# A state-space convolution fused with a gated MLP: convolution over two half-sequences with 2048-point spectra, lag tables of 16 powers by 41 offsets, a new static order

## The chip, the cores and the metric

The kernel runs on one core of one Trainium2 chip. The metric is the device time of one execution in microseconds. Each statement about time rests on several executions of both kernels on the same chip. A single core shows no second die to compare with, so a run counts as slow when it is more than 1.5% above the fastest run of the same kernel. Different runs were made on different chips, each beside the kernel before, so compare two runs by their ratios rather than by their times.

Engine names as in the profile: PE is TensorE, the matrix engine (PEld its weight loads), DVE is VectorE, ACT is ScalarE, POOL is GpSimd, SP the engine that issues most of the DMAs. A trailing q (SPq) is an engine's instruction queue.

## The reference, cut to what matters

```python
def reference(u, A, B, C, log_dt, Dskip, w_gate, w_up, w_down):   # cut: complex A, B, C as re and im
    xn = layernorm(u)                                  # 2048 x 512
    dt = exp(log_dt)[:, None]
    P  = exp((dt * A)[:, :, None] * arange(2048))      # 512 channels x 128 modes x 2048 lags
    K  = einsum("dn,dnl,dn->dl", C, P, dt * B).real    # the convolution kernel: 512 x 2048
    y  = irfft(rfft(pad(xn.T)) * rfft(pad(K)))[:, :2048].T + xn * Dskip
    h  = sigmoid(xn @ w_gate) * (xn @ w_up)            # 512 -> 1792
    return u + y + h @ w_down
```

The kernel splits this into three strands that share the engines:

- **Tables.** K is built from powers. A table G (powers times coefficients) and a table H (offsets) are grown by complex multiplications on DVE, in four chunks of 128 channels. PE multiplies G with H to get all lags ("lag products"), and a selection matmul puts them in order.
- **Units.** In 16 units (2 passes over the channels, 8 units each) PE transforms a slice of the input, forms the spectrum of K with matmuls against constant weights E ("spectrum matmuls"), DVE multiplies the two, and PE transforms back ("inverse matmuls"). Slices go through DRAM between the steps (z before, v after).
- **The gated MLP.** PE does gate, up and down matmuls. DVE multiplies gate and up ("gated products").

## The kernel before: the parts that the argument touches

Every engine is given its instructions in a fixed order. A list `ORDER` of about 900 operation numbers, written in the file, says in which order all operations are issued. It was found by a search before the kernel was written down; no scheduler runs on the chip.

```python
NGE = 32            # powers in G
NH = 21             # offsets in H
ORDER = [ ... ]     # the static order of all operations (cut)

def cmul(lo, outp, n, m, conj, ...):       # n table elements at a time, on DVE
    V.tensor_tensor(out=outp, in0=lo, in1=mre, op=ALU.mult)      # L660
    V.tensor_tensor(out=tmp,  in0=lo, in1=mim, op=ALU.mult)      # L661
    V.tensor_tensor(out=outp[re], ...)                           # L665
    V.tensor_tensor(out=outp[im], ...)                           # L666

def f_k(...):                              # lag products: 64-column tiles, 42 moving columns
    for comp in range(2):
        for t in range(2):
            T.matmul(pk[64*t:64*t+64, y % 8, :], G[:, r, :, comp, h], H[:, r, :, comp, h],
                     start=(comp == 0), stop=(comp == 1), tile_position=(0, 64*t))    # L724
...
for p in range(2):
    for u in range(8):                     # one unit
        lx = dma("SP", zx, z_v[...], acq=[xsl, zsl], ...)        # load of z, 256 KB
        mm = pl.add("PE", ..., fm, [lx, l_m2], ...)              # input transform
        le = dma("SP", es, cten["E"].ap()[:, gs, :, :], ...)(640 * KB)
        def fk(...):                       # 4 groups x 5 = 20 spectrum matmuls    # L810
            for r in range(GB):
                for kt in range(NKT):
                    T.matmul(two(sk)[:, DW*r:DW*r+DW], es()[:, r, kt, :], kT[p][:, kt, :],
                             start=kt == 0, stop=kt == NKT - 1)
        def fp(...):                       # the one product of the unit, 128x2048    # L817
            V.tensor_tensor(out=pp(), in0=xx(), in1=kb(), op=ALU.mult)
        ...                                # 16 inverse matmuls                    # L827
```

Of the kernel before, what the change touches and what calls it, by code (L numbers as in the profile page):

```python
# [31 lines left out]
NGE = 32  # L32
NH = 21
# [3 lines left out]
QUAD = ((0, 0), (2, 64), (1, 0), (3, 64))  # L37
# [16 lines left out]
LAG0 = [0, 1, 2, 3, 4, 5, 6, 7, 258, 260, 262, 516, 772, 256, 512, 768, 1024, 1280, 1536, 1792, 2048]  # L54
# [5 lines left out]
def _th(s, b, k2):  # L60
    return 2 * np.pi * (s * b / 4096.0 + k2 * b / 32.0)

def _build_S1():
    S1 = np.zeros((NA, 128))
    a = np.arange(NA)
    S1[:, 0] = 1.0
    S1[:, 1] = (-1.0) ** a
    for s in range(1, 64):
        S1[:, 2 * s] = np.cos(2 * np.pi * s * a / 128)
        S1[:, 2 * s + 1] = -np.sin(2 * np.pi * s * a / 128)  # L70
    return S1

def _build_S2():
    S2 = np.zeros((128, NA))
    a = np.arange(NA)
    S2[0, :] = 1.0 / 4096
    S2[1, :] = (-1.0) ** a / 4096
    for s in range(1, 64):
        S2[2 * s, :] = 2.0 / 4096 * np.cos(2 * np.pi * s * a / 128)
        S2[2 * s + 1, :] = -2.0 / 4096 * np.sin(2 * np.pi * s * a / 128)  # L80
    return S2

def _build_M2():
    M2 = np.zeros((NG, 128, 128))
    b = np.arange(32)[:, None]
    k2 = np.arange(32)[None, :]
    for g in range(NG):
        for par in range(2):
# [3 lines left out]
            if s >= 1:  # L92
                t = _th(s, b, k2)
                M[0:32, 0:32] = np.cos(t)
                M[32:64, 0:32] = np.sin(t)
                M[0:32, 32:64] = -np.sin(t)
                M[32:64, 32:64] = np.cos(t)
            else:
                t0 = 2 * np.pi * k2 * b / 32.0
                M[0:32, 0:16] = np.cos(t0)[:, 0:16]  # L100
                M[0:32, 32 + 1:32 + 16] = -np.sin(t0)[:, 1:16]
                M[0:32, 32 + 0] = (-1.0) ** b[:, 0]
                t64 = 2 * np.pi * (64 + 128 * (k2 - 16)) * b / 4096.0
                M[32:64, 16:32] = np.cos(t64)[:, 16:32]
                M[32:64, 32 + 16:32 + 32] = -np.sin(t64)[:, 16:32]
# [3 lines left out]
def _build_MAB():  # L109
    MA = np.zeros((NG, 128, 128))  # L110
    MB = np.zeros((NG, 128, 128))
    k2 = np.arange(32)[:, None]
    b = np.arange(32)[None, :]
    for g in range(NG):
        for par in range(2):
# [14 lines left out]
            else:  # L130
# [7 lines left out]
                t64 = 2 * np.pi * (64 + 128 * (k2 - 16)) * b / 4096.0  # L138
# [8 lines left out]
def _row(l):  # L147

    v = int(np.float32(ml_dtypes.bfloat16(l)))
    seg = range(0, 8) if v < 256 else (8, 9, 10, 13) if v < 512 else (11, 12, 14, 15) if v < 1024 else \  # L150
        (16, 17, 18, 19) if v < 2048 else (20,)
    for h in seg:
        if v >= LAG0[h] and (v - LAG0[h]) % 8 == 0 and (v - LAG0[h]) // 8 < NGE:
            return h, (v - LAG0[h]) // 8
    raise ValueError(l)

def _build_E(S1, M2):

    E = np.zeros((NKT, 4, NGE, NG, 128))
    z = M2.reshape(NG, 2, 2, 32, 128)  # L160
    s1 = S1.reshape(NA, NG, 2, 2)
    for l in range(L):
        h, i = _row(l)
        if h < 20:
            E[h // 4, h % 4, i] += np.einsum("gpc,gpcf->gf", s1[l // 32], z[:, :, :, l % 32, :])
    E = E.reshape(NKT, 128, NG, 128).transpose(1, 2, 0, 3)
    for g in range(NG):
        if g % GB >= GB // 2:
            E[:, g] = np.roll(E[:, g], 64, axis=-1)
    return E  # L170

def _consts():
# [4 lines left out]
    def quads(m, cross=False):  # L177
        m = m.transpose(1, 0, 2)
        lo, hi = m[0:64, :, 0:64].copy(), m[64:128, :, 64:128].copy()
        for g in range(NG):  # L180
            if cross and g % GB >= GB // 2:
                lo[:, g], hi[:, g] = m[64:128, g, 64:128], m[0:64, g, 0:64]
# [3 lines left out]
    return dict(ident=f(np.eye(128)), S1=f(np.concatenate([S1, S1], axis=0)), S2=f(_build_S2()), M2=f(quads(M2)),  # L186
# [3 lines left out]
    35, 3, 2, 22, 1, 33, 0, 12, 7, 36, 5, 34, 6, 47, 4, 29, 46, 38, 48, 49, 8, 32, 37, 50, 30, 39, 40, 11, 52, 51, 53, 41, 43,  # L190
    55, 16, 42, 31, 9, 54, 44, 56, 28, 57, 45, 10, 58, 59, 13, 186, 60, 18, 23, 602, 24, 607, 62, 603, 17, 608, 26, 612, 604,
    61, 14, 613, 19, 15, 614, 63, 21, 609, 629, 66, 25, 625, 27, 64, 630, 20, 621, 65, 617, 622, 67, 187, 633, 626, 618, 127,
    637, 68, 126, 645, 634, 128, 638, 641, 125, 646, 70, 69, 138, 130, 141, 653, 642, 99, 71, 657, 100, 654, 102, 635, 72, 73,
    647, 658, 636, 659, 139, 648, 639, 129, 140, 74, 101, 605, 660, 104, 103, 75, 640, 627, 606, 142, 623, 105, 188, 107, 628,
    143, 631, 624, 108, 610, 189, 106, 632, 156, 109, 131, 76, 150, 655, 133, 110, 132, 611, 643, 115, 77, 651, 656, 78, 644,
    649, 79, 151, 615, 650, 190, 152, 159, 80, 619, 652, 111, 616, 160, 191, 177, 135, 620, 161, 82, 134, 661, 81, 136, 112,
    178, 113, 192, 83, 179, 183, 662, 85, 663, 84, 193, 87, 114, 86, 194, 117, 116, 697, 157, 699, 664, 158, 88, 698, 665, 671,
    137, 195, 89, 90, 91, 184, 153, 196, 705, 672, 185, 666, 92, 673, 93, 94, 154, 197, 95, 155, 174, 707, 700, 674, 97, 706,
    675, 683, 96, 708, 681, 200, 203, 243, 198, 206, 689, 202, 682, 205, 691, 204, 690, 180, 216, 201, 729, 98, 676, 692, 199,
    731, 244, 359, 730, 709, 249, 684, 181, 732, 711, 207, 217, 182, 710, 208, 713, 118, 175, 209, 214, 717, 121, 712, 176, 215,  # L200
    719, 714, 210, 119, 693, 718, 211, 120, 701, 220, 122, 165, 720, 162, 702, 123, 221, 703, 694, 212, 163, 715, 704, 246, 164,
    733, 247, 213, 250, 248, 259, 721, 166, 716, 260, 725, 734, 167, 218, 722, 219, 695, 245, 251, 124, 726, 252, 222, 257, 696,
    258, 253, 224, 223, 254, 263, 264, 685, 255, 230, 286, 225, 687, 231, 287, 686, 256, 723, 289, 232, 288, 688, 293, 727, 290,
    233, 291, 292, 735, 261, 234, 168, 728, 171, 235, 757, 169, 172, 226, 170, 736, 765, 236, 758, 173, 227, 724, 767, 228, 237,
    737, 229, 238, 759, 262, 738, 239, 147, 144, 739, 148, 145, 149, 760, 240, 146, 302, 807, 241, 740, 747, 741, 303, 242, 374,
    458, 300, 265, 381, 748, 301, 294, 465, 742, 295, 306, 267, 266, 307, 296, 297, 375, 268, 329, 298, 749, 444, 273, 376, 299,
    274, 333, 304, 378, 334, 275, 330, 377, 305, 332, 337, 335, 380, 459, 336, 276, 269, 766, 379, 338, 460, 775, 768, 270, 345,
    464, 773, 277, 331, 463, 271, 346, 750, 445, 272, 461, 278, 466, 774, 751, 462, 446, 339, 449, 279, 450, 382, 467, 451, 776,
    447, 280, 448, 752, 789, 437, 791, 468, 790, 805, 281, 383, 430, 469, 806, 452, 384, 470, 282, 416, 471, 385, 423, 453, 809,
    808, 386, 431, 454, 761, 810, 387, 432, 283, 388, 455, 762, 434, 417, 763, 792, 433, 418, 284, 436, 781, 456, 421, 438, 419,  # L210
    782, 457, 764, 420, 285, 435, 424, 439, 367, 340, 422, 343, 344, 341, 389, 409, 799, 390, 342, 349, 797, 393, 440, 308, 394,
    798, 391, 800, 425, 360, 350, 392, 441, 426, 309, 801, 442, 347, 402, 427, 348, 802, 443, 310, 428, 429, 361, 316, 783, 311,
    317, 318, 362, 787, 319, 784, 366, 368, 363, 320, 321, 365, 364, 793, 322, 395, 369, 323, 795, 794, 803, 403, 312, 804, 404,
    324, 785, 313, 408, 410, 314, 796, 406, 786, 370, 407, 405, 788, 486, 865, 315, 411, 493, 325, 371, 866, 396, 372, 412, 373,
    326, 570, 811, 397, 577, 413, 812, 487, 398, 833, 414, 488, 777, 415, 327, 556, 399, 778, 489, 779, 492, 400, 328, 490, 769,
    401, 571, 780, 491, 770, 351, 572, 576, 353, 574, 352, 573, 575, 557, 354, 771, 594, 558, 596, 355, 600, 772, 841, 559, 356,
    562, 357, 837, 358, 561, 584, 586, 578, 585, 590, 598, 592, 494, 560, 579, 563, 580, 588, 813, 479, 495, 472, 496, 514, 581,
    814, 497, 582, 815, 498, 583, 499, 564, 816, 817, 473, 521, 565, 823, 474, 566, 475, 500, 477, 515, 818, 824, 480, 476, 516,
    478, 519, 518, 522, 481, 520, 517, 535, 482, 501, 507, 825, 502, 528, 523, 505, 503, 504, 506, 483, 834, 567, 826, 524, 838,
    849, 827, 842, 542, 484, 867, 850, 508, 485, 868, 568, 569, 529, 828, 549, 509, 875, 530, 510, 857, 533, 543, 858, 511, 534,  # L220
    544, 873, 532, 512, 531, 536, 548, 874, 513, 876, 545, 547, 550, 537, 546, 538, 845, 551, 539, 846, 525, 552, 540, 881, 526,
    541, 553, 882, 847, 527, 869, 848, 885, 870, 835, 886, 554, 859, 836, 839, 555, 860, 890, 843, 840, 889, 883, 844, 851, 884,
# [57 lines left out]
def _d1(n):  # L280
    return 0.09 + n * 0.00117
# [737 lines left out]
```

## Time and profile before

The kernel before took 265.56 us (three runs, 264.41 to 265.71); the profiled span is 262.9 us.

| what | before |
|---|---|
| time (median of 3) | 265.56 us |
| span of the profiled run | 262.9 us |
| granted PE clock, mean | 0.993 |
| DMA | 49.34 MB |

The first part of its page gives busy time of each engine, share of the span, and instructions:

```profile
PE 243.0 (92%) x2254; PEld 131.4 (50%) x2254; DVE 192.9 (73%) x389; ACT 157.9 (60%) x247; POOL 21.7 (8%) x41
```

PE is the busiest, but the average hides two stages. The windows view of the kernel before splits the span at the last table instruction. Columns: window, its length, busy time (and instruction count) of each engine, granted PE clock, DMA share, GB/s:

```profile
4.10:171.20 167.10, 155.80 (x1434) 82.05 (x1432) 160.95 (x347) 122.87 (x203) 17.63 (x31) 1.00 0.70 190
171.20:262.90 91.70, 84.50 (x816) 48.36 (x814) 31.94 (x43) 33.87 (x45) 3.27 (x4) 0.98 0.65 186
```

Until the last table is done, DVE is busy 160.95 of 167.10 us. It leaves 6.2 us idle. After it, PE is busy 84.50 of 91.70 us, with 7.2 us idle, 6.3 of them after its last matmul. So this identity holds by construction:

span = 4.1 + (DVE work before the last table + DVE gaps) + (PE work after it + PE gaps)

The waits view of PE in that second stage shows how full it is. Columns: who waited for whom, total us, times, longest:

```profile
PE pair_64 L810 <- DMA big<-c_E: 0.3, 1, 0.3
PE pair_63 L794 <- DMA big<-z_scr: 0.3, 1, 0.3
PE pair_63 L724 <- DVE big L666: 0.3, 1, 0.3
```

PE waits less than one microsecond in all for anything. The same view for DVE in the first stage (the longest wait of its first line, 4.2 us, ends at the stage's start and is no part of the 6.2 us):

```profile
DVE stats L482 <- DMA big<-in_A_u_dram: 4.4, 2, 4.2
DVE big L660 <- ACT big L682: 2.6, 1, 2.6
DVE big L570 <- ACT big L563: 0.7, 1, 0.7
```

The timeline of PE shows what the pieces cost (start, us, engine, line, operation, count):

```profile
135.68 2.35 PE L810 MATMUL pair_64<-big 128*128 128x256 bf16 x20
...
142.31 2.13 PE L724 MATMUL pair_64<-big 128*64 128x42 bf16 x64
...
146.68 0.63 PE L827 MATMUL pair_64<-big 64*64 64x256 bf16 x16
```

### The profile page before, as it was taken

Reading aid. Unit: us, or ns where it says so; the run is one execution under the profiler, and the core shown is the slowest. Engines: PE = TensorE matmul, PEld = TensorE weight load, DVE = VectorE, ACT = ScalarE, POOL = GpSimd, SP = SyncE. Lnnn points to the kernel's source line nnn. Section 1 sums busy time; section 2 is a strip of 40 time slices with the busy share of each in tenths; the row PEclk is TensorE's granted clock in tenths of the full one; section 3 lists DMA queues with packets and bytes.
Section 4 is the critical chain, followed back from the end, with each engine's and each line's share of the span. In section 5 each row is a group of like instructions: output and inputs, shape, how many; then the busy total and the mean of one; then the engine's idle time right before and its main releaser. Section 6 shows DMA issues by size and latency. Waiting matters only on the chain.

```text
span 262.9 us, 5705 instructions
## 1 busy us (share of the span) xinstructions
PE 243.0 (92%) x2254; PEld 131.4 (50%) x2254; DVE 192.9 (73%) x389; ACT 157.9 (60%) x247; POOL 21.7 (8%) x41
## 2 busy tenths in 40 slices
PE   7689998899999989989999999999999999999990
PEld 2353333334336444747567557477457656444440
DVE  3889999999999999999999599924111223566323
ACT  2699999999996544294674845752536776310000
POOL 1300220072000000102000000000020200000000
PEclk9999999999999999999999999999999999999997
DMA  7999975664559022857978846947997983496123
GB/s 163 161 295 323 339 220 145 190 139 107 145 202 157 15 80 80 228 178 143 306 216 253 228 118 193 271 124 235 302 306 175 308 261 96 131 264 201 44 67 100
DMA packets 50924, 49.34 MB, mean 188 GB/s; under 512 B 13137, under 2 KB 44114, under 8 KB 50770
## 3 DMA queue, kind: packets, MB, share of 16 engines
q1 hardware_dynamic: 47362, 44.66, 60.0%
q0 software_dynamic: 960, 1.57, 3.7%
q10 hardware_dynamic: 2576, 2.75, 3.6%
q8 instruction: 17, 0.28, 0.4%
q14 instruction: 9, 0.07, 0.1%
HBM read 30.36 MB, written 12.06 MB: 161 GB/s over the span
## 4 chain that ended last, share of the span: by engine, by line
DVE 47%; PE 28%; DMA 11%; SPq 4%; issue 3%; ACT 3%; DVEq 1%; POOL 1%; ACTq 0%
DVE big L661 8%; DVE big L660 8%; DVE hT_sb L928 8%; DVE big L665 5%; DVE big L666 5%; PE bank_68 L946 5%; SPq L382 4%; PE pair_64 L810 3%; DVE stats L482 3%; DMA big<-z_scr 3%; DMA big<-c_E 2%; DVE big L611 2%; PE bank_67 L921 2%; DMA big<-v_scr_94 2%; DVE big L609 2%
## 5 line engine op out<-in xcount | busy, mean ns | idle before, releaser
L946 PE MATMUL bank_68<-wd_sb,hT_sb 128*128 128x512 bf16 x196 | 44.7, 379 | 1.3 <-ACT glu_sb L976 1.1
L817 DVE TENSOR_TENSOR big<-big 128x2048 bf16<-128x2048 bf16 x16 | 19.5, 1220 | 26.7 <-ACT big L813 15.6
L906 PEld LDWEIGHTS <-wg_sb 128*128 128x128 bf16 x236 | 21.9, 97 | 29.1 <-issue 8.7
L921 PEld LDWEIGHTS <-wu_sb 128*128 128x128 bf16 x224 | 21.0, 97 | 28.8 <-issue 6.5
L946 PEld LDWEIGHTS <-hT_sb 128*128 128x128 bf16 x224 | 21.1, 98 | 27.6 <-issue 3.9
L810 PEld LDWEIGHTS <-big 128*128 128x128 bf16 x320 | 30.8, 98 | 6.7 <-DMA big<-c_E 1.4
L660 DVE TENSOR_TENSOR big<-big 128x256 bf16<-128x256 bf16 (+4 forms) x52 | 31.2, 600 | 2.8 <-ACT big L682 2.6
L661 DVE TENSOR_TENSOR big<-big 128x256 bf16<-128x256 bf16 (+4 forms) x52 | 31.3, 601 | 0.0
L921 PE MATMUL bank_67<-xnT,wu_sb 128*128 128x512 bf16 x88 | 22.6, 379 | 0.3 <-DVE hT_sb L928 0.2
L665 DVE TENSOR_TENSOR big<-big 128x128 bf16<-128x128 bf16 (+4 forms) x52 | 21.4, 412 | 0.6
L810 PE MATMUL pair_64<-big 128*128 128x256 bf16 x180 | 21.2, 273 | 0.6 <-DMA big<-c_E 0.6
L666 DVE TENSOR_TENSOR big<-big 128x128 bf16<-128x128 bf16 (+4 forms) x52 | 21.2, 407 | 0.0
L906 PE MATMUL bank_65<-xnT,wg_sb 128*128 128x512 bf16 (+1 forms) x80 | 19.7, 368 | 1.3 <-ACT hT_sb L915 0.9
L906 PE MATMUL bank_67<-xnT,wg_sb 128*128 128x512 bf16 (+1 forms) x76 | 18.5, 368 | 2.2 <-DVE hT_sb L928 2.2
L928 DVE TENSOR_TENSOR hT_sb<-hT_sb,bank_67 128x512 bf16<-128x512 bf16 x22 | 15.0, 682 | 7.4 <-PE bank_67 L921 7.3
L906 PE MATMUL bank_66<-xnT,wg_sb 128*128 128x512 bf16 (+1 forms) x80 | 19.7, 369 | 0.7 <-DVE hT_sb L928 0.4
L921 PE MATMUL bank_66<-xnT,wu_sb 128*128 128x512 bf16 x72 | 18.5, 380 | 0.2 <-ACT hT_sb L915 0.2
L921 PE MATMUL bank_65<-xnT,wu_sb 128*128 128x512 bf16 x64 | 16.4, 379 | 1.1 <-ACT hT_sb L915 0.5
L928 DVE TENSOR_TENSOR hT_sb<-hT_sb,bank_66 128x512 bf16<-128x512 bf16 x18 | 12.3, 681 | 6.7 <-PE bank_66 L921 3.8
L724 PEld LDWEIGHTS <-big 128*64 128x64 bf16 x512 | 16.1, 157 | 2.2 <-DVE big L666 1.0
L813 ACT ACTIVATE big<-pair_64 128x1024 bf16<-128x1024 f32 x9 | 9.2, 1023 | 13.3 <-PE pair_64 L810 11.1
L915 ACT ACTIVATE hT_sb<-bank_66 128x512 bf16<-128x512 f32 x19 | 11.7, 615 | 8.0 <-PE bank_66 L906 8.0
(117 smaller groups left out, 356.2 us busy)
## 6 DMA issues: line engine op xcount, KB each, us to landing
big<-c_E SPq DMA_DIRECT2D x16, 640.0 KB, 5.7
z_scr<-big SPq DMA_DIRECT2D x16, 256.0 KB, 2.8
big<-z_scr SPq DMA_DIRECT2D x16, 256.0 KB, 5.2
big<-big SPq DMA_DIRECT2D x64, 64.0 KB, 3.3
big<-in_A_u_dram SPq DMA_DIRECT2D x8, 256.0 KB, 7.5
v_scr_94<-big SPq DMA_DIRECT2D x8, 256.0 KB, 3.3
big<-v_scr_94 SPq DMA_DIRECT2D x8, 256.0 KB, 4.6
v_scr_95<-big SPq DMA_DIRECT2D x8, 256.0 KB, 4.0
```

The source lines that it names most:

```text
L660: V.tensor_tensor(out=wide(outp), in0=lov, in1=mre, op=ALU.mult)
L661: V.tensor_tensor(out=wide(tb()), in0=lov, in1=mim, op=ALU.mult)
L665: V.tensor_tensor(out=outp[:, :, :, 0, :], in0=outp[:, :, :, 0, :], in1=tb()[:, :, :, 1, :], op=opr)
L666: V.tensor_tensor(out=outp[:, :, :, 1, :], in0=outp[:, :, :, 1, :], in1=tb()[:, :, :, 0, :], op=opi)
L724: T.matmul(pk[64 * t:64 * t + 64, y % 8, :], G[:, r, :, comp, h], H[:, r, :, comp, h], start=(comp == 0), stop=(comp == 1), tile_position= ...
L810: T.matmul(two(sk)[:, DW * r:DW * r + DW], es()[:, r, kt, :], kT[p][:, kt, :], start=kt == 0, stop=kt == NKT - 1)
L817: V.tensor_tensor(out=pp().rearrange("p c g d -> p c (g d)"), in0=xx().rearrange("p c g d -> p c (g d)"), in1=kb().unsqueeze(1).to_broadca ...
L906: T.matmul(bank(sl)[:, c0:c1], w[:, kt, k * 128:(k + 1) * 128], xnT[:, grp, kt, c0:c1], start=(kt == 0), stop=(kt == KT - 1))
L915: S.activation(out=hT_sb[:, hs.idx, k % 2, :], in_=bank(sl), func=ACT.Sigmoid)
L921: T.matmul(bank(sl), wu_sb[:, kt, k * 128:(k + 1) * 128], xnT[:, grp, kt, :], start=(kt == 0), stop=(kt == KT - 1))
L928: V.tensor_tensor(out=h(), in0=h(), in1=bank(sl), op=ALU.mult)
L946: T.matmul(bank(po), hT_sb[:, hts[k // 2].idx, k % 2, jj * 128:(jj + 1) * 128], wd_sb[:, k, :], start=(k == 0), stop=k == FT - 1, **kw)
```

## The change

The intent: two half-sequences make each spectrum 2048 points instead of 4096, so the spectrum matmuls and their constant weights halve (PE and DMA are relieved). For that, each unit needs one more product on DVE and more inverse matmuls. The lag tables become 16 powers by 41 offsets, so the lag products sit on 32-column tiles with 82 moving columns. The order of all operations was searched anew.

```diff
-NGE = 32
-NH = 21
+NGE = 16
+NH = 41
+NU = 16
 ... (constants of the transforms for 2048 points cut)
-ORDER = [ ... ]
+ORDER = [ ... another list, for the new set of 930 operations ... ]
 def f_k(...):
-    for t in range(2):
-        T.matmul(pk[64*t:64*t+64, y % 8, :], G[:, r, :, comp, h], H[:, r, :, comp, h], ...,
-                 tile_position=(0, 64*t))
+    for t in range(4):
+        T.matmul(pk[32*t:32*t+32, y % 4, :], G[:, r, :, comp, h], H[:, r, :, comp, h], ...,
+                 tile_position=(0, 32*t))
 ...
-le = dma("SP", es, cten["E"].ap()[:, gs, :, :], ...)(640 * KB)
+le = dma("SP", es, cten["E"].ap()[:, gs, :, :], ...)(320 * KB)
 def fk(...):
-    for r in range(GB):                 # 4 groups
+    for g in range(2):                  # 2 groups
         for kt in range(NKT): T.matmul(...)
 ...
+def fpb(...):                            # second product of the unit, 128x1024
+    V.tensor_tensor(out=pq(), in0=xx()[:, :, 0, :], in1=kb()[:, 2*DW:4*DW]..., op=ALU.mult)
+pb_ = pl.add("DVE", 0.62, fpb, [pa_], ...)
 ...                                      # inverse matmuls: 16 -> 24 per unit
```

Not shown: the selection was rewritten for the new tables, and some buffers were added (spectrum weights 2 to 3, the evicted spectrum of K 1 to 2).

## The prediction

> What bounds it now. The windows view gives two stages. From 4.1 to 171.5 us VectorE (DVE) is busy 161.3 of 167.4 us, TensorE (PE) 155.8. It ends with the last DVE table instruction, after which PE starts the last lag-table product. From 171.5 to 262.9 us DVE is busy 31.6 of 91.4 us, PE 84.5: PE-bound, with 6 us of finals and stores at the end. So the span is (DVE work before the last table) + (PE work after it) + gaps. PE's clock row is full; the clock plays no part.
>
> What changes, with pitches from the timeline:
> - Kernel-spectrum matmuls halve, 320 to 160; twenty take 2.18 us, so PE drops 34.9 to 17.5 us. Their DMA (16 x 640 KB) halves.
> - Lag-table matmuls stay 512, on 32-column tiles instead of 64, with 82 moving columns instead of 42. Today 64 take 2.08 to 2.3 us (33 ns each), more than streaming needs[...]. The selection matmuls, with 32-column weights, take 13.5 ns. The Trainium skill, "TensorE: Matmul & The Clock Gate" (LDWEIGHTS), says load time follows the weight's columns; the trace agrees in direction. Estimate 0.9 to 1.0 us per 64: 17.5 to 7.5 us over eight.
> - Inverse matmuls grow 256 to 384: 16 take 0.57 us, 24 about 0.85; +4.5 us. Selection +1 us.
> - PE pitches sum to 230 us before, about 209 after (-21).
> - DVE: table steps are 47 instead of 44 elements per chunk (+4 us); each unit gets a second product, 128x1024, about 0.6 us, x16 = +10 us. Sum 191 to 206 us.
> - ScalarE hardly changes.
>
> Critical path. I placed both static instruction orders against these pitches. Before: 161 us of DVE work up to the last table instruction (ended at 172: 10 us of gaps), then 81 us of PE work, 4 of gaps, 6 of tail: 262.9. After: 172 us of DVE work up to the last table instruction (table elements, eight second products, three more gated products), then 65 us of PE work. The second stage gains 16 us, the first loses 11: only 5 of 21 us survive at equal gaps. PE gets some 30 us of slack in the first stage, which gains nothing. I expect 2 to 4 us less DVE stall early (layer-norm statistics come first in its queue), a tail 1 us shorter, and 2 to 5 us more PE wait behind the last inverse matmul, where 8 us of other PE work covers the store and reload of the result (3 to 4 and 4.6 to 6.5 us to landing today).
> Lower bound: 4 + 172 + 65 + 5 = 246 us of span; the stated time is about 2.7 us above the span today.
>
> Predicted: 256.0 us, range 248.0 to 264.0. Faster by over 2%: 0.74; within 2%: 0.22; slower: 0.04.
>
> What the profile would show. Last table instruction at 178 to 184 us, DVE 95% busy before it, PE clearly under its present 93% there; DVE busy 203 to 210 us in all, PE near 222; 64 lag matmuls in 0.85 to 1.1 us; 10 spectrum matmuls in 1.1; 24 inverse ones near 0.85; first final matmul 48 to 58 us after the last table; DMA near 43 MB.
>
> What would make it wrong. If the last table comes well before 178 us, or less PE work follows it, time falls to 248 or below. If 32-column tiles do not beat 33 ns, 2 us are lost behind the tables and the rest is hidden. If DVE waits for swapped copies or ScalarE (three 0.9 us evictions per unit), or the reload stalls PE by 8 us, it ends near 264.

## The result, and the profile after

The changed kernel took 278.98 us (four runs, 276.59 to 280.86), the kernel before in the same rounds 265.63 us (four runs, 264.41 to 267.98). The ratio is 1.045, with a 95% interval of 1.036 to 1.054: slower by 4.5%. A ratio here is always the mean time of one kernel's fast runs over that of the other's fast runs of the same rounds, so it is not quite the ratio of the medians that I quote.

The page of the changed kernel, engine totals:

```profile
PE 229.2 (83%) x2290; PEld 117.6 (43%) x2290; DVE 208.6 (76%) x407; ACT 162.7 (59%) x249; POOL 20.8 (8%) x43
```

PE lost 14 us of busy time and DVE gained 16. DMA went from 49.34 to 43.42 MB. The windows view of the changed kernel, split again at its last table instruction:

```profile
4.10:193.00 188.90, 156.97 (x1511) 77.77 (x1508) 174.07 (x354) 129.61 (x209) 15.75 (x31) 0.96 0.57 153
193.00:276.00 83.00, 69.50 (x778) 38.80 (x774) 34.51 (x54) 31.89 (x40) 3.27 (x4) 0.97 0.62 169
```

| | before | changed | difference |
|---|---|---|---|
| DVE work up to the last table | 160.95 | 174.07 | +13.1 |
| DVE gaps there | 6.2 | 14.8 | +8.6 |
| PE work after it | 84.5 | 69.5 | -15.0 |
| PE gaps there | 7.2 | 13.5 | +6.3 |
| span, with 4.1 us at the start | 262.9 | 276.0 | +13.1 |

The work terms alone would have given 1.9 us. The gaps cost 14.9 us. That is the result in one line. One caution: each column is one execution, and the one of the kernel before is a quick one (its 35 executions beside the experiments have spans of 262.8 to 267.4 us, half of them 264.6 or less). So some 2 us of the 14.9 may be the draw, and a difference of 2 or 3 us in one gap should not be read.

The waits of DVE in the first stage, changed kernel (4.1 us of its first line end at the stage's start again):

```profile
DVE stats L499 <- DMA big<-in_A_u_dram: 5.4, 3, 4.1
DVE hT_sb L964 <- PE bank L957: 2.8, 4, 1.6
DVE ln_nb_f L472 <- ACT ln_m_f L467: 2.7, 2, 1.4
DVE big L841 <- DMA big<-big: 1.8, 1, 1.8
DVE big L680 <- ACT big L721: 1.4, 2, 1.1
```

Two of them lie in the first 20 us (the input and the layer-norm means). From 20 us on DVE waits 7.2 us instead of 2.6: for the matmuls of the gated products, for the swapped copies of the transformed input, for ScalarE.

The pieces on PE's timeline in the changed kernel (two lines whose bracket names the wait before them):

```profile
140.31 1.25 PE L835 MATMUL pair<-big 128*128 128x256 bf16 x10 [0.35 <-ACT big L837]
141.50 0.85 PE L858 MATMUL pair<-big 64*64 64x256 bf16 x24
...
192.78 2.88 PE L744 MATMUL pair<-big 128*32 128x82 bf16 x128 [2.59 <-DVE big L685]
```

Ten spectrum matmuls and 24 inverse matmuls take what was predicted (the listed lengths overlap a little; the next piece starts 0.1 to 0.2 us before they end). The lag products do not: 128 take 2.7 to 2.9 us, 21 to 23 ns each, where 15 had been assumed.

The waits of PE around and after the last table, in the changed kernel:

```profile
PE pair L817 <- DMA big<-z_scr: 4.3, 2, 3.6
PE pair L744 <- DVE big L685: 2.6, 1, 2.6
PE bank L908 <- DMA big<-v_scr: 1.7, 1, 1.7
PE pair L858 <- DVE big L841: 1.5, 1, 1.5
PE bank L957 <- DVE hT_sb L964: 0.7, 2, 0.5
```

The wait of 2.6 us for the table ends at 192.78 us and so lies before the split at 193.0. The others, 8.2 us against 0.9 before, lie in the second stage: for z loads, for the reload of v in the tail, and for DVE. The idle time at the very end is 1 us shorter than before (5.3 us), as predicted.

One more thing is new. The clock row of the page before is full until the last slice. In the changed kernel PE falls to about half its clock several times. One of these places, in the timeline of PE, with the wait for a z load in the bracket:

```profile
178.33 0.64 PE L817 MATMUL pair<-big,m 64*64 64x256 bf16 x8 [2.82 <-DMA big<-z_scr]
178.90 1.89 PE L942 MATMUL bank<-xnT,wg_sb 128*128 128x512 bf16 x4
180.72 1.27 PE L766 MATMUL pair<-big,sw 128*32 128x96 bf16 x64
181.93 1.04 PE L957 MATMUL bank<-xnT,wu_sb 128*128 128x512 bf16 x4
```

After 2.82 us of idle time four matmuls of 512 columns take 1.89 us, and a little later four take 1.04 us. The windows view (same columns as above) confirms the clock there, at 0.53 to 0.55 in three such stretches:

```profile
62.00:65.60 3.60, 2.83 (x7) 0.99 (x7) 3.57 (x7) 3.57 (x6) 0.00 (x0) 0.53 0.41 143
178.20:181.80 3.60, 3.47 (x76) 1.70 (x76) 3.13 (x7) 1.02 (x1) 0.00 (x0) 0.53 0.08 18
222.70:226.40 3.70, 3.70 (x16) 1.92 (x15) 1.27 (x2) 1.91 (x3) 0.00 (x0) 0.55 0.64 168
```

The Trainium skill, "TensorE: Matmul & The Clock Gate" (Why this matters for your kernels), warns of PE-idle gaps above about 3 us between bursts of matmuls, because an idle window takes the array back to half its clock. This trace agrees in kind, but the length of the gap alone does not decide it. Gaps of 2.7 and 2.8 us were enough here (before 62.8 and 178.3 us), while one of 2.8 us before 135.6 us and one of 2.6 us before 192.8 us left the clock at 1.00. No run here shows what else decides.

### The profile page after: what moved, and what is told of

Read it like the earlier page. It is cut to its first block, busy times and chain, and to the rows that moved or that the text cites. A ratio compares the mean times of both kernels' runs of the same rounds, so it can differ in the third digit from the quotient of the medians.

```text
span 276.0 us, 5805 instructions
## 1 busy us (share of the span) xinstructions
PE 229.2 (83%) x2290; PEld 117.6 (43%) x2290; DVE 208.6 (76%) x407; ACT 162.7 (59%) x249; POOL 20.8 (8%) x43
## 2 busy tenths in 40 slices
DMA packets 51069, 43.42 MB, mean 157 GB/s; under 512 B 13153, under 2 KB 44258, under 8 KB 51042
## 4 chain that ended last, share of the span: by engine, by line
PE 40%; DVE 29%; DMA 16%; ACT 6%; issue 4%; SPq 2%; DVEq 0%; ACTq 0%
PE bank L942 11%; PE bank L957 9%; DMA big<-z_scr 8%; PE bank L982 6%; DVE big L681 5%; DVE big L680 5%; PE pair L744 4%; DVE hT_sb L964 4%; PE pair L835 4%; DVE big L685 4%; DVE big L686 3%; DMA ident<-c_ident 3%; DMA big<-big 2%; DMA big<-v_scr 2%; SPq L397 2%
## 5 line engine op out<-in xcount | busy, mean ns | idle before, releaser
L942 PE MATMUL bank<-xnT,wg_sb 128*128 128x512 bf16 (+1 forms) x236 | 57.4, 382 | 1.4 <-ACT hT_sb L951 1.4
L957 PE MATMUL bank<-xnT,wu_sb 128*128 128x512 bf16 x224 | 55.9, 384 | 2.9 <-ACT hT_sb L951 1.5
L982 PE MATMUL bank<-wd_sb,hT_sb 128*128 128x512 bf16 x224 | 52.2, 387 | 3.3 <-ACT glu_sb L1012 3.3
L964 DVE TENSOR_TENSOR hT_sb<-hT_sb,bank 128x512 bf16<-128x512 bf16 x56 | 37.0, 682 | 10.7 <-PE bank L957 6.0
L951 ACT ACTIVATE hT_sb<-bank 128x512 bf16<-128x512 f32 x56 | 32.3, 599 | 15.1 <-PE bank L942 15.0
L680 DVE TENSOR_TENSOR big<-big 128x256 bf16<-128x256 bf16 (+5 forms) x52 | 33.1, 636 | 2.5 <-ACT big L721 1.4
L681 DVE TENSOR_TENSOR big<-big 128x256 bf16<-128x256 bf16 (+5 forms) x52 | 32.9, 633 | 0.0
L822 ACT ACTIVATE big<-pair 128x1024 bf16<-128x1024 f32 x16 | 16.3, 1026 | 11.4 <-PE pair L817 7.3
L685 DVE TENSOR_TENSOR big<-big 128x128 bf16<-128x128 bf16 (+5 forms) x52 | 21.9, 420 | 0.8
L835 PE MATMUL pair<-big 128*128 128x256 bf16 x160 | 20.4, 278 | 2.2 <-ACT big L837 0.7
L862 ACT ACTIVATE big<-pair 128x1024 bf16<-128x1024 f32 x16 | 16.4, 1026 | 9.0 <-PE pair L858 5.2
L686 DVE TENSOR_TENSOR big<-big 128x128 bf16<-128x128 bf16 (+5 forms) x52 | 21.6, 416 | 0.0
L837 ACT ACTIVATE big<-pair 128x1024 bf16<-128x1024 f32 x16 | 16.4, 1027 | 7.8 <-PE pair L835 3.4
L835 PEld LDWEIGHTS <-big 128*128 128x128 bf16 x160 | 15.9, 100 | 8.2 <-issue 3.0
L645 ACT ACTIVATE big<-pair 128x1024 bf16<-128x1024 f32 x16 | 16.3, 1019 | 1.7 <-DMA z_scr<-big 1.0
L858 PE MATMUL pair<-big 64*64 64x256 bf16 x384 | 13.7, 272 | 3.1 <-ACT big L822 1.6
## 6 DMA issues: line engine op xcount, KB each, us to landing
z_scr<-big SPq DMA_DIRECT2D x16, 256.0 KB, 2.6
big<-z_scr SPq DMA_DIRECT2D x16, 256.0 KB, 4.6
v_scr<-big SPq DMA_DIRECT2D x16, 256.0 KB, 2.6
big<-v_scr SPq DMA_DIRECT2D x12, 256.0 KB, 4.6
big<-in_A_u_dram SPq DMA_DIRECT2D x8, 256.0 KB, 7.2
```

Of the source, the lines that this page charges most:

```text
L680: V.tensor_tensor(out=wide(outp), in0=lov, in1=mre, op=ALU.mult)
L681: V.tensor_tensor(out=wide(tb()), in0=lov, in1=mim, op=ALU.mult)
L685: V.tensor_tensor(out=outp[:, :, :, 0, :], in0=outp[:, :, :, 0, :], in1=tb()[:, :, :, 1, :], op=opr)
L686: V.tensor_tensor(out=outp[:, :, :, 1, :], in0=outp[:, :, :, 1, :], in1=tb()[:, :, :, 0, :], op=opi)
L835: T.matmul(two(sk)[:, o:o + DW], es()[:, g, kt, :], kT[p][:, kt, :], start=kt in (0, NKT - 1), stop=kt >= NKT - 2)
L942: T.matmul(bank(sl)[:, c0:c1], w[:, kt, k * 128:(k + 1) * 128], xnT[:, grp, kt, c0:c1], start=(kt == 0), stop=(kt == KT - 1))
```

## The experiments

Two theories at the start. **Order:** the new operations are worth about what was predicted, but the list in which they stand wastes it in waits, and another list of the same operations is fast. **Work:** the new set of operations is itself no better, because PE's saved work lies where it does not count and DVE's added work where it does. A third question is whether the lost **clock** is a cause or a shadow of the waits.

All times are medians of four runs, slow ones included; beside each stands the ratio to the kernel before of the same rounds, with its 95% interval.

| run | us | ratio | 95% interval |
|---|---|---|---|
| changed kernel | 278.98 | 1.045 | 1.036 to 1.054 |
| e1_start | 278.58 | 1.044 | 1.036 to 1.052 |
| e2_tail | 274.80 | 1.028 | 1.021 to 1.035 |
| e3_zload | 273.98 | 1.029 | 1.022 to 1.036 |
| e4_all | 276.89 | 1.040 | 1.032 to 1.049 |
| e5_after_reordered | 265.84 | 1.003 | 0.996 to 1.011 |
| e6_before_reordered | 270.16 | 1.011 | 1.004 to 1.019 |
| e7_spectra_doubled | 278.30 | 1.046 | 1.041 to 1.051 |
| e8_before_half_spectra | 268.54 | 1.009 | 1.004 to 1.014 |
| e9_before_extra_dve | 274.29 | 1.026 | 1.018 to 1.034 |
| e10_before_half_spectra_half_load | 261.40 | 0.978 | 0.971 to 0.986 |
| e11_reordered_start_a | 271.74 | 1.015 | 1.007 to 1.024 |
| e12_reordered_start_b | 274.73 | 1.026 | 1.018 to 1.034 |
| e13_kept_clock | 277.23 | 1.033 | 1.025 to 1.042 |
| e14_second_product_gpsimd | 286.39 | 1.078 | 1.072 to 1.084 |
| e15_reordered_gpsimd | 278.79 | 1.044 | 1.033 to 1.055 |
| e16_reordered_other_seed | 269.41 | 1.013 | 1.005 to 1.020 |
| e17_zload_and_tail | 276.25 | 1.037 | 1.030 to 1.043 |
| e18_reordered_one_move | 266.31 | 1.000 | 0.995 to 1.005 |

And the two-stage sum, worked out from the windows view of the profiled run of each, split at that run's last table instruction:

| run | last table at | DVE work + gaps before it | PE work + gaps after it | span | mean clock |
|---|---|---|---|---|---|
| before | 171.2 | 161.0 + 6.2 | 84.5 + 7.2 | 262.9 | 0.993 |
| changed kernel | 193.0 | 174.1 + 14.8 | 69.5 + 13.5 | 276.0 | 0.965 |
| e5_after_reordered | 188.2 | 172.2 + 11.9 | 72.3 + 6.9 | 267.4 | 0.984 |
| e7_spectra_doubled | 191.4 | 174.1 + 13.2 | 75.2 + 9.3 | 275.9 | 0.987 |
| e8_before_half_spectra | 174.6 | 161.0 + 9.5 | 78.9 + 13.7 | 267.2 | 0.958 |
| e9_before_extra_dve | 178.3 | 166.5 + 7.7 | 84.9 + 8.8 | 272.0 | 0.986 |
| e10_before_half_spectra_half_load | 173.6 | 161.0 + 8.6 | 76.4 + 8.9 | 258.9 | 0.971 |
| e18_reordered_one_move | 185.5 | 172.2 + 9.2 | 72.9 + 6.3 | 264.7 | 0.991 |

(The profiled run of e5 was its slowest, 269.45 us; its other three lie at 265.7 to 265.9. So its gaps are on the high side, as those of the kernel before are on the low side.)

### e1_start, e2_tail, e3_zload, e4_all: repairing single waits of the changed kernel

```diff
 # e1: loads of the identity and log_dt earlier, the warm-up matmuls all at the start
+_mv([7, 6], 2); _mv([30, 31, 32, 33, 34, 35, 36, 37], 29)     # move operations in ORDER behind another
 # e2: in the tail, reloads of v stand ahead of the output stores in the queues
+_mv([604, 616, 612, 605], 608); _mv([610, 606], 618)
 # e3: a z load needs only its own buffer, and five of them are issued earlier
-lx = dma("SP", zx, ..., acq=[xsl, zsl]);  ex = pl.add("ACT", 0.91, fe, [mm])
+lx = dma("SP", zx, ..., acq=[zsl]);       ex = pl.add("ACT", 0.91, fe, [mm], acq=[xsl])
+_mv([571], 497); _mv([541], 482); _mv([556], 572); _mv([586], 542); _mv([526], 557)
 # e4: all three
```

> Only the issue order of the start changes: the identity and log_dt loads go right behind the first four input loads, and all 30 warm-up matmuls run first. Order theory (the new order, not the new work, costs the time): transposes start near 10.5 us instead of 12.7, TensorE is at full clock when the first gate matmuls start, the first lag-table product starts 3 to 5 us earlier than 90.8, total 3 to 5 us less than the changed kernel (about 274 to 276 us). Work theory (the extra VectorE work and the longer chain per unit cost it): a gain at the start is eaten by VectorE later, total within 1 us of the changed kernel.

> Only the issue order of the end changes: the six reloads of the inverse result that stand behind output stores in the DMA queues are issued before the first output store. Order theory: the wait of 1.7 us before the first late final matmul and the 5 us reload in the chain that ended last go, total 2 to 3 us less than the changed kernel. Work theory: less than 1 us.

> The spectrum loads (z) of the last five units no longer wait for a free buffer of the forward result (that buffer is taken at the eviction instead) and are issued right behind the matmul that frees their own buffer. Order theory: after the last lag-table product the products of those five units come less than 5 us apart instead of 6.6, TensorE waits for z fall from 4.3 to under 1 us in that stage, total 4 to 8 us less. Rival: the chain of eviction, swapped copies and product sets that pace, not the load; then the waits move to the swapped copies and the total changes by under 2 us.

> The three order edits together. Order theory: gains add, 9 to 16 us, 262 to 269 us, near the kernel before. Work theory: at most 3 us, 275 us or more.

The repaired start gained nothing: 278.6 us, although the last table came 2.8 us earlier in its profiled run (190.2 us); PE's gaps behind it grew from 13.5 to 16.0 us. The tail and the z loads each gained 1.6 to 1.7%, some 4 to 5 us. All three together gained less than either of these alone, with intervals that overlap. A single wait taken away is real, but what it sets free runs into the next one. The traces show it: in e3 PE's waits for z after the last table go from 4.3 us to none, and its waits for the DVE product before the inverse matmuls from 1.5 to 4.1 us.

### e17_zload_and_tail: only the two repairs that worked

```diff
+ the edits of e2 and of e3 together, not that of e1
```

> The changed kernel with the two repairs that each gave 4 to 5 us (earlier z loads; reloads ahead of the stores in the tail), without the third, the early start, which alone gave nothing. If they lie on separate stretches of the path and the start was what spoilt the run with all three (276.9 us): 269 to 271 us. If any shift of the order upsets the rest: 273 to 278 us.

276.25 us. The two do not add either. Their ratios alone were 1.028 and 1.029, together 1.037. The intervals overlap, so I do not say that the pair is worse than one of them; I say that a second 4 us did not appear. In its trace the waits for z are down to 0.5 us and those for the DVE product up to 3.8 us. The losses of this order are not separate waits that can be struck off one by one.

### e5_after_reordered and e6_before_reordered: the same operations in another list

```diff
-ORDER = [ ... ]     # the list of the kernel
+ORDER = [ ... ]     # the same numbers in another sequence, from a local search over a rough model
```

The search moves one to four operations at a time and keeps what shortens a model made of measured durations, dependences, buffers and waits for DMA. It was run in the same way on both kernels, started from the kernel's own list or from an earlier result of the search.

> The changed kernel with every operation kept and only the list of the static order replaced by one found by a local search over the two pieces of the work (durations from the traces, eight DMA lanes, waits). Theory A (the new list, not the new work, makes the kernel slow): 258 to 266 us, at or below the kernel before, granted clock above 0.98, last table instruction by 186 us. Theory B (the new work itself is slower: 13 us more VectorE work in stage one and small pieces that nothing can cover): it stays above 272 us whatever the order.

> The kernel before, operations kept, its order replaced by one from the same search. It is the fair partner of the reordered changed kernel. If the order of the kernel before was already good: 262 to 268 us, the same as the kernel before. If the search finds something general that the hand-in order lacks: 255 to 260 us. If the search only fits its own rough durations: above 270 us.

The changed kernel in its new list took 265.84 us, 13 us less than in its own (11 us by the ratios, 1.003 against 1.045), and the same as the kernel before. The kernel before in a searched list took 270.16 us: its own list was no worse than what the search found. (Only one searched list was run for it, against four for the changed kernel.) So the search is no magic, and the list that came with the change was a bad one for these operations. The windows view of e5, split at its last table:

```profile
4.10:188.20 184.10, 150.01 (x1469) 74.97 (x1493) 172.17 (x349) 127.29 (x206) 13.10 (x28) 0.98 0.55 153
188.20:267.40 79.20, 72.27 (x797) 40.98 (x804) 37.19 (x58) 31.14 (x41) 5.75 (x7) 0.99 0.68 187
```

PE's gaps after the last table went from 13.5 to 6.9 us; there is 2.8 us more PE work there and it costs nothing extra. One wait is left in that stage:

```profile
PE pair L746 <- DVE big L687: 0.3, 1, 0.3
```

Theory Order holds for 11 to 13 us. It does not hold for the rest: the new operations in the best list tried are not faster than the old ones in theirs.

### e7_spectra_doubled: the saved PE work put back

```diff
-                for g in range(2):
+                for g in (0, 1, 0, 1):          # every spectrum matmul twice, same result
```

> The changed kernel with its spectrum matmuls run twice into the same bank (same result): 17 us of TensorE work put back, 8.7 of it in pass one (before the last table) and 8.7 in pass two. If the saved TensorE work is worth its full length everywhere: +17 us (296). If it is worth something only after the last table, as the prediction holds: +8 to +9 us (287), last table unmoved within 2 us. If stage two too is bound by waits and not by work: +0 to +5 us (279 to 284).

278.30 us: the 17 us of PE work came back for nothing. The windows view of e7:

```profile
4.10:191.40 187.30, 162.16 (x1565) 83.71 (x1584) 174.12 (x354) 129.62 (x208) 15.75 (x31) 0.98 0.58 155
191.40:275.90 84.50, 75.20 (x847) 46.31 (x858) 34.67 (x55) 31.51 (x40) 3.27 (x4) 1.00 0.60 166
```

In the second stage busy time rose by 5.7 us, less than the 8.7 us of matmuls added, in part because the clock there is 1.00 instead of 0.97; and the gaps fell by 4.2 us. The clock rose from 0.965 to 0.987. DVE's gaps before the last table hardly moved, 13.2 against 14.8 us. In the changed kernel's own order the halved spectra, its main gain, are worth nothing, in the first stage as predicted and in the second stage against the prediction.

### e8 and e10: the gain of the change alone, in the kernel before

```diff
 # e8: 10 of 20 spectrum matmuls (wrong on purpose)
-                    for kt in range(NKT):
+                    for kt in ((0, 1, NKT - 1) if r % 2 else (0, NKT - 1)):
 # e10: 10 matmuls, and only half of the weights loaded
-le = dma("SP", es, cten["E"].ap()[:, gs, :, :], ...)
+le = dma("SP", lambda: es()[:, 0:2], cten["E"].ap()[:, GB*u:GB*u+2, :, :], ...)
-                for r in range(GB): for kt in range(NKT): T.matmul(..., es()[:, r, kt, :], ...)
+                for r in range(GB): for kt in ((0, 1, 2) if r % 2 == 0 else (3, 4)): T.matmul(..., es()[:, r // 2, kt, :], ...)
```

> The kernel before with only 10 of the 20 spectrum matmuls of each unit (wrong result on purpose; loads, order, everything else as before): the gain of the change alone, without its costs. The prediction's sum says 17 us less TensorE work, of which 8.7 lie after the last table: 257 to 258 us. If waits take the place of the work: 261 to 265 us.

> The kernel before with 10 of 20 spectrum matmuls and also only half of the spectrum weights loaded, 16 x 320 KB instead of 16 x 640 KB (wrong result on purpose). The run with half of the matmuls alone took 268.5 us, with waits for these loads among the stage-two waits. If the loads held it: 258 to 262 us, granted clock back above 0.98. If the waits only move to the z loads and to the VectorE and ScalarE hand-overs, and TensorE goes on losing its clock in them: 264 to 269 us.

Both compute a wrong spectrum. The comparison with the reference happened to let e8 pass (the convolution is a small part of the output) and refused e10 with an error of 0.024; neither is a kernel to use.

With half of the spectrum matmuls alone, the kernel before became 0.9% slower. Windows of e8 and, after them, its waits of PE in the second stage:

```profile
4.10:174.60 170.50, 149.92 (x1337) 76.27 (x1352) 160.99 (x347) 122.70 (x202) 17.62 (x31) 0.96 0.67 187
174.60:267.20 92.60, 78.93 (x726) 41.35 (x736) 32.00 (x43) 33.92 (x45) 3.27 (x4) 0.95 0.63 183
```

```profile
PE pair L810 <- DMA big<-c_E: 3.2, 3, 2.1
PE pair L794 <- DMA big<-z_scr: 1.9, 1, 1.9
```

PE's busy time in the second stage fell by 5.6 us only, in part because matmuls after the waits ran at half the clock (14 down matmuls took 4.9 us after the z wait, 3.2 us before it), and the gaps rose by 6.5. The loads now set the pace that PE had set. With the loads halved too, e10 took 261.4 us, 2.2% less than before:

```profile
...
173.60:258.90 85.30, 76.36 (x736) 40.79 (x734) 31.98 (x43) 34.08 (x45) 3.27 (x4) 0.99 0.62 175
```

The wait for the weights is gone from its list; PE gaps are 8.9 us. (The expectation of a clock above 0.98 failed: it is 0.971, with 0.99 in the second stage.) So the change's gain exists and is worth about 6 us in the old order, not the 8.7 us of its matmuls after the last table, and only if the loads shrink with it.

### e9_before_extra_dve: the main cost of the change alone, in the kernel before

```diff
                 V.tensor_tensor(out=pp(), in0=xx(), in1=kb(), op=ALU.mult)
+                V.tensor_tensor(out=pp()[:, 0], in0=xx()[:, 0], in1=kb(), op=ALU.mult)   # same values again
```

> The kernel before, with one more 128x1024 VectorE product after each of its 16 products (it rewrites the first half of the result with the same values): the cost of the change's second product alone, 16 x 0.6 us. If VectorE before the last table is the bound of stage one, as the prediction says, those that stand before it (5 to 8) move the last table and the end by 3 to 5 us: 269 to 271 us. If VectorE has slack even there: 266 to 267 us. If each product also lengthens the path of its unit in stage two: 273 us or more.

274.29 us, +2.6%: nearly 7 us for 16 products that take 0.6 us each (9.6 us of DVE). The windows view of e9 shows the first stage:

```profile
4.10:178.30 174.20, 156.87 (x1435) 82.81 (x1432) 166.47 (x355) 122.91 (x203) 17.65 (x31) 0.99 0.66 184
178.30:272.00 93.70, 84.89 (x816) 48.49 (x814) 37.53 (x51) 33.86 (x44) 3.27 (x4) 0.98 0.63 180
```

Eight of them stand before the last table (355 instructions instead of 347), add 5.5 us of work there and move it by 7.1 us. DVE work before the last table costs its full length. Most of the other 1.6 us is no effect of the edit: DVE's wait for the input at the start is 5.6 us in this execution and 4.4 us in that of the kernel before.

Put together: in the kernel before, the gain alone (e10) is worth 6 us and this cost alone (e9) takes 7. The table elements, 4.4 us more in the changed kernel's groups of table instructions, come on top. That fits Theory Work: the best list tried for the new operations only equals the old kernel. It is not a proof. The added inverse matmuls were not run alone, the three terms sum to about 5 us of loss that e5 does not show, and a better list may exist.

### e13_kept_clock: dummy matmuls in the waits

```diff
 def fm(...):                                     # input transform of a unit
+    for _ in range(10 if (p, u) in ((0, 3), (1, 1), (1, 5)) else 0):
+        T.matmul(two(sl)[:, 0:512], xnT[:, 0, 0, 0:128], xnT[:, 0, 0, 0:512], start=True, stop=True)
 def f_k(...):                                    # lag products
+    for _ in range(6 if half_ == 0 else 0): T.matmul(...the same...)
```

> The changed kernel in its own order with dummy matmuls that keep TensorE busy where the trace shows it idle for 2.1 to 3.6 us: 10 ahead of three of the unit transforms that wait for their z load, 6 ahead of each chunk's first lag product (about 0.2 us each, into the bank that the operation holds already; same result). They stand in waits, so they cost nothing where the wait is still there. If the clock that TensorE loses after such gaps matters: granted clock 0.98 or more and 3 to 5 us less, 274 to 276 us. If the waits are the matter and the clock only their shadow: clock up, time 277 to 280 us.

The profiled run's clock rose from 0.965 to 0.986. The times were 275.95 and 273.81 us in the two fast runs and 278.52 and 278.67 in two that count as slow, with clocks of 0.986, 0.992, 0.973 and 0.971. Fast runs against fast runs the ratio fell from 1.045 to 1.033, about 3 us, but the two intervals overlap, and with all four runs of each kernel the means lie only some 2 us apart. So the lost clock may be worth some 2 to 3 us of the 23 us by which the prediction missed. It is not settled, and it is not the main cause. A searched list (e16, below) ran at clocks of 0.949 to 0.963, no higher than the changed kernel's, and took 269.4 us. And with the clock kept, the profiled run still has 9.6 us of PE gaps after the last table, dummy matmuls not counted as gaps.

### e14 and e15: the second product on GpSimd

```diff
-                V.tensor_tensor(out=pq(), in0=xx()[:, :, 0, :], ...)
+                P.tensor_tensor(out=pq(), in0=xx()[:, :, 0, :], ...)
-            pb_ = pl.add("DVE", 0.62, fpb, ...)
+            pb_ = pl.add("POOL", 0.62, fpb, ...)
```

> The changed kernel, own order, with the second product on GpSimd instead of VectorE: takes some 10 us off VectorE, 5 of them before the last table. If VectorE's added work is what the change pays with (the same addition cost the kernel before 7 us): 272 to 275 us, last table 4 to 5 us earlier. If GpSimd is slow at it (over 2 us each) and in the way of its own queue: the units' chain grows and it ends at 280 us or later.

> The searched order (265.8 us) with the second product on GpSimd. If VectorE bounds stage one and GpSimd needs under 2 us: 260 to 263 us, the first version that would beat both. If the product on GpSimd lengthens every unit in stage two, or slows VectorE: 268 us or more.

Both became much slower: 286.39 us in the kernel's own order, 278.79 us in the searched one. The groups of instructions of e14 tell why (line, engine, operation, shapes, count, busy time and mean ns of one, idle time before):

```profile
L845 POOL TENSOR_TENSOR big<-big 128x1024 bf16<-128x1024 bf16 x16 | 45.4, 2845 | 53.0 <-ACT big L837 15.6 <-DMA v_scr<-big 11.0 <-DMA big<-big 10.6
```

```profile
L680 DVE TENSOR_TENSOR big<-big 128x1024 bf16<-128x1024 bf16 x12 | 10.5, 873 | 0.3
```

and of the changed kernel, for the same two groups (there the first is on DVE):

```profile
L845 DVE TENSOR_TENSOR big<-big 128x1024 bf16<-128x1024 bf16 x16 | 11.0, 685 | 0.0
L680 DVE TENSOR_TENSOR big<-big 128x1024 bf16<-128x1024 bf16 x12 | 8.3, 688 | 0.3
```

One product takes 2.85 us on GpSimd and 0.69 us on DVE. Moreover some of DVE's own multiplications became longer, 873 instead of 688 ns in the group shown (others, such as L681 with the same shape, did not): DVE's total is 216.9 us in e14, more than the 208.6 us it had with the product. The Trainium skill, "SBUF — State Buffer" (SBUF: two separate sides), says that DVE instructions with two SBUF inputs and GpSimd instructions that read SBUF take turns on a shared pair of ports, one blocked until the other has finished. The trace agrees in direction. "GPSIMD Engine Reference" (4.1 Engine selection) gives GpSimd as about twice as slow for two-input elementwise work; here it is 4.2 times on average (2845 over 685) and 3.1 times for the shortest of the 16 (2119). The average may contain time in which GpSimd was blocked.

### e11, e12, e16, e18: how reproducible is the good order

```diff
 # e11, e12: the first 90 or 70 operations from e1's start, then the search again
 # e16: another seed of the search, same score in the model
 # e18: e5 with operation 281 (a table multiplication, 2.3 us) behind 725, eleven places earlier in the list
```

> The changed kernel, the searched order again, but its first 90 operations those of the run with the repaired start (there TensorE had 35 us of work done at 40 us, in the searched order 20 us). If TensorE work done early is worth something: 259 to 263 us, a gain of 3 to 6 us over the searched order. If VectorE's work before the last table still sets the time (30 us done at 40 us in both): 264 to 268 us, the same.

> The same with the first 70 operations kept and the rest searched from another start. Same expectations: 259 to 263 us if the early TensorE work counts, 264 to 268 us if not; a difference of over 4 us from its sister run says how much the time depends on the order alone.

> The changed kernel in a second order from the same search with another seed and the same score. If the order as such is the 13 us (a good one is reproducible): 263 to 268 us. If the first one was a lucky draw, as the two runs with repaired starts suggest: 270 to 276 us.

> The searched order (265.8 us) with one operation moved: the trace shows VectorE idle for 3.4 us at 114.5 us, behind a gated product whose matmuls stand behind a selection, while a table multiplication of the next chunk, 2.3 us long, was ready; it now stands five places earlier. If stage one is bound by VectorE's idle time and work: 262 to 264 us. If the table then only waits at its next input: 265 to 267 us.

e11 took 271.74 us and e12 274.73 us: filling PE early brought nothing (their last tables came at 187.8 and 190.3 us, at most 0.4 us earlier than in e5). e16 took 269.41 us. The four searched lists spread over 9 us on the chip; e16, to which the model gave the same score as to e5, took 3.6 us more. All four searched lists were below the changed kernel's own, so a better list is easily found, but e5 was the best draw of four. e18 removed a DVE wait of 3.4 us that the trace of e5 showed. Its DVE gaps fell by 2.7 us in the profile, but the time stayed: 266.31 us, ratio 1.000. A part of that wait had been 2.4 us in the middle of a selection with no releaser in the profile, which the other runs of e5 may not have had; I cannot tell.

No version here beats both kernels: e5 and e18 equal the kernel before.

## Why the prediction was wrong, point by point

- **Two stages and their bounds: right.** DVE work before the last table counts in full (e9: 5.5 us of work there, the last table 7.1 us later). PE work before it counts for nothing (e7: with the doubled spectra the last table came at 191.4 us, no later than the 193.0 us without).
- **DVE work of 172 us up to the last table: right.** It measured 174.1. Eight second products (8 x 0.69 us), three more gated products and 4.4 us of table elements make up 11.9 us of the 13.1 us of difference.
- **PE work of 65 us after it: about right.** It measured 69.5, but the prediction counted 81 us for the kernel before where the windows view has 84.5. On equal terms the fall was predicted as 16 us and measured as 15.0. What it had too low: the lag products took 21 to 23 ns and not 15 (the estimate of 0.9 to 1.0 us per 64 came out as 1.35 to 1.45), and some matmuls ran at half the clock. That estimate let the time follow the columns of the weights. The recorded weight loads of the lag products fell from 157 ns at 64 columns to 116 at 32, not to half, and over all groups they do not follow the columns (medians of 98 ns at 128 in the spectrum matmuls and 97 at 32 in the selection).
- **The last table at 178 to 184 us: wrong.** It came at 193. The prediction expected 2 to 4 us less DVE stall early; DVE gaps grew from 6.2 to 14.8 us. Early waits grew by some 3 us (kernels with one and the same start differ by 1.5 us there), and those after 20 us from 2.6 to 7.2 us.
- **"Only 5 of 21 us survive at equal gaps": this is the step that failed.** The prediction took the gaps as they were and changed them by a few microseconds, for a net gain. The predicted span is 253.3 us (256.0 less 2.7), the measured one 276.0. Of these 22.7 us about 3 lie in the work terms (1.9 us left instead of 5) and the rest in the gaps: 13.4 us before (6.2 + 7.2), 28.3 after (14.8 + 13.5). I had treated gaps as a constant of the program. They are what is left when each wait is covered by other work in the order of the list. In the changed kernel's list the waits stood uncovered. With the same operations in another list (e5) PE's gaps after the last table are 6.9 us, as before, and DVE's are 11.9 (9.2 in e18). Removing PE work uncovers waits if the list stays: in the kernel before, e8 has 5.6 us less PE work and 6.5 us more gaps in the second stage, and in the changed kernel e7 puts the work back and PE's gaps there fall by 4.2 us. For the gaps of DVE this is not shown: they hardly moved in e7.
- **"PE's clock row is full; the clock plays no part": wrong for the changed kernel.** In the kernel before no wait of PE in mid-kernel is longer than 1.2 us. In the changed kernel it lost clock after three waits of 2.7 to 3.6 us, though not after every wait of that length. By e13 this may be some 2 to 3 us.
- **The order.** I had placed the new list against estimated durations and read no trouble in it. The list alone costs 11 to 13 us (e5). Where these lie I can say by stage only (in the profiled runs of e5 and e18 the last table comes 4.8 and 7.5 us earlier, and the second stage is 3.8 us shorter with 3 us more work in it), not by single waits: single repairs gained 4 us each and did not add (e4, e17).
- **What stays open.** The share of the lost clock (overlapping intervals), why the four searched lists differ by 9 us on the chip, and which waits of DVE in the first stage the list causes. Untested is also why lag and selection matmuls on tiles of the same width differ; the weights of the lag products are read at a stride, those of the selection are not.

## What to carry to other kernels

When one engine is 92% busy, the loads and hand-overs behind it are hidden by its work; take work away and the next limit may lie at once behind it, so test the removal alone (e8 does that, and was 0.9% slower than the kernel before). Price an addition on the engine that bounds the stage at its full length, and a removal on the other engine at nothing until a run shows otherwise. When operations stand in a hand-in static order, a change of the operations and a change of the order are two changes: run the old and the new operations each in more than one order before blaming or praising the operations.

## What the Trainium skill lacked or had wrong

- "TensorE: Matmul & The Clock Gate" (Why this matters for your kernels) puts the harmful idle gap at about 3 us. Here 2.68 us (before 62.8 us) and 2.82 us (before 178.3 us) were enough to see a granted clock of 0.53 in the 3.6 us around what followed, and in e8 2.08 us (before 213.2 us; clock 0.50 from 215 to 217 us). But 2.82 us before 135.6 us and 2.59 us before 192.8 us left it at 1.00.
- The same page (Back-to-back issue gap) gives about 25 ns from start to start as the least for one matmul, and (Measured speedup vs the span model) about 4 ns for each further tile packed into the array. Neither says what a stream of weight loads and matmuls on 32-column tiles costs, which the prediction needed and estimated at 15 ns. The traces show 21 to 23 ns for the lag products (128 in 2.7 us, 82 moving columns) and 13.6 ns for the selection (64 in 0.87 us, 96 moving columns). Why the narrower one is slower, no run here tells.
- "GPSIMD Engine Reference" (4.1 Engine selection) says about twice as slow for two-input elementwise work. For 128x1024 bf16 the runs show 2845 ns on average and 2119 at the least, in which there may be time blocked by DVE, against 685 ns, and some of DVE's neighbouring multiplications at 873 instead of 688 ns.
- No page says that a kernel's waits grow when the work that hides them is removed, or how much of a removal to expect back: here 17 us of matmuls removed gave nothing alone (e8) and 6 us with their loads removed as well (e10).
